# Twelve sign rows per head in place of 64 one-hot pattern rows in a bucketed attention kernel

## The chip, the core and the metric

The kernel runs on one core of a Trainium2 chip. The metric is the device time of one execution in microseconds. Three runs of the kernel before gave 800.62 us as their median (800.1 to 803.21).

## The reference

Attention with a hash mask, then a mixture of experts on its output. Query and key of a head are projected on six vectors; the signs make a bucket number, and a query sees the keys of its own bucket only. A query that finds no key in its bucket has every score at -1e9, and so the softmax is the mean over all keys.

```python
batch, n_heads, seq, head_dim = (4, 8, 768, 64)
q_bits = (einsum('bhsd,dk->bhsk', q, proj) > 0)      # 6 bits
k_bits = (einsum('bhsd,dk->bhsk', k, proj) > 0)
mask = q_bucket[:, :, :, None] == k_bucket[:, :, None, :]
scores = where(mask, scale * q @ k.T, -1000000000.0)
attn = exp(scores - max) / (sum + 1e-09)
out = attn @ v
# then the experts: route every row to its best one of 8, relu(x @ w1[e]) @ w2[e], times the gate
```

## The kernel before

The 32 heads go in 16 pairs (`NPR`); two heads share most instructions. Every pair needs four operand tiles per head, 128 rows by 768 columns: `m1` and `s1` (in 64 of the rows the rounded query or key, in the other 64 the mask rows) and `m2` and `s2` (the rounded values and the residues that the rounding left). A score is two matmuls into one bank: `s1` by `m1` (product and mask together) and `s2` by `m2` (the cross terms), lines 301 and 302 in `scores`. Three sets of operand tiles (`gens`) go round.

While pair i is scored, three other things are woven into TensorE's order. `maxp(i+1)` (lines 240 and 246) multiplies `s1` by `m1` of the next pair once without the residues, VectorE takes the maximum over the keys (lines 242, 248), and `maxp_back` (lines 269 to 272) transposes the maxima back and adds them to the mask rows of `m1`. `turn(i+2)` (line 175) transposes query and key of the pair after the next into a `psx` bank, ScalarE rounds them into `m1` (line 182), VectorE takes the residues (line 190), one ScalarE copy (line 193) and three DMAs (lines 194 to 196) bring them to the other rows. `signs(i+2)` projects on the six vectors: eight matmuls (line 208) of 384 columns into four row groups of a bank, and one VectorE comparison per half makes the bits (line 210). `patterns(i+2)` turns the bits into 64 rows: for each half and head one bf16 matmul by the constant `pat` (line 223), then a copy into the 64 mask rows of `m1` (line 224, on VectorE or ScalarE) and a ScalarE Relu into those of `s1` (line 225). A row of `m1` is then 0 where it is the query's bucket and far below zero elsewhere, a row of `s1` one-hot.

TensorE's order is written out by hand: the strings `PLAN` (six rows, one for each block of 128 keys of pair i), `PLAN0` (the first pair) and `FIRST` (before it). S is a third of the scores of a block, M a step of `maxp`, T the next step of the chain `turn`, `signs`, `patterns`, and P the last step of `patterns` of the pair before. The other queues are ordered by a scheduler. `ps_x` has two banks (`psx`), which transposes, signs, patterns and several others share. SP issues the loads and copies in order.

Of the kernel before, what the change touches and what calls it, by code (L numbers as in the profile page):

```python
# [25 lines left out]
BIG = 2.0 ** 100  # L26
CFG = dict(spd=(15,), fxs=3, wy=(0.3, 0.71), hpf=0, he=0, hn=0, hm=0, avp=(1, 2, 3, 4, 5, 6), avs=(2,), early=2, w3=(0, 0.9), x3=(0, 1), nmd=1, man=(), man0=2, hpo=0, hpe=0, p0=(0, 1), p1=(0, 0.25), p2=(0, 0.4), p3=(0.4, 0.9), s0=4, rc='DDDD', rq=(1, 2), tq=(3, 3, 1, 1, 0, 0), wh=(0.5, 0.78), ws=(0.78, 1.05), n2=2, psx=2, psm=2, pss=2, npb=6, ut=8, qk=4, v=2, wm=(0, 0.9), wf=(0.04, 1.02), wx=(0.3, 0.71), sub="DPPD", fx='D', fx3='R', raw=4, wp=7, LS=4, LL=7, pn=8, rv=(0,), rs='DDPP', r1=(0, 0.5), r2=(0, 1), avg=1, fub=2, fd=2, pm=(), fj=0, fxe=1.0)
# [4 lines left out]
    "yMSTPSMSM",  # L32
# [3 lines left out]
    "SFTTTfEMSfMSMTF",  # L36
    "fSMSMMETBABSe",
# [4 lines left out]
    "SMMSSMT",  # L42
    "TMSSMS",
    "MTMlSMBTSSMMT",
    "SABSMS",
)
FIRST = "UtmmUmtmmmttmtmUtmtnnnnbnUbnUnUnUnbUUb"


def host_consts():  # L50
    beta = (np.arange(64)[None, :] >> np.arange(6)[:, None]) & 1
    pat = np.zeros((128, 2, 128), np.float32)
    for h in range(2):
        r = 64 * h
        pat[r:r + 6, h, 0:64] = (2 * beta - 1) * BIG
        pat[r + 6, h, 0:64] = 6 * BIG
        pat[r + 32:r + 38, h, 64:128] = 2 * beta - 1
        pat[r + 38, h, 64:128] = 4
    return {
        "c_pat": pat,  # L60
        "c_id": np.eye(128, dtype=np.float32),
        "c_tri": np.triu(np.ones((128, 128), np.float32), 1),
    }
# [20 lines left out]
def attention(ctx, actx, tc, a, x_d, l_d, route=None, setup=None, before_last=None):  # L84
# [51 lines left out]
    pat = const.tile([P, 2, P], BF16, name="pat")  # L136
    pat32 = sm.tile([P, 2, P], F32, name="pat32", bufs=1)
    nc.sync.dma_start(out=pat32, in_=a["c_pat"])
    zst = const.tile([P, 32], F32, name="zst")
    nc.gpsimd.memset(zst, 0.0)  # L140
    bits = []
    for j in range(2):
        bt = const.tile([P, S], BF16, name=f"bits{j}")
        nc.gpsimd.memset(bt, 0.0)
        bits.append(bt)
    nc.vector.tensor_copy(out=zst[:, 0:6], in_=pr)
    nc.vector.tensor_copy(out=pat, in_=pat32)
# [51 lines left out]
    def signs(i, heads=(0, 1)):  # L199

        t = st[i]
        bt = bits[(i + heads[0]) % 2]
        rows = slice(64 * heads[0], 64 * heads[-1] + 64)
        for half in range(2):
            hs = slice(half * HALF, (half + 1) * HALF)
            z = ps_x.tile([P, MAIN], F32, name="psx")
            for o in range(2 * heads[0], 2 * heads[-1] + 2):
                nc.tensor.matmul(z[32 * o:32 * o + 32, 0:HALF], zst, (t["m2"], t["s2"])[o % 2][o // 2][:, hs].bitcast(F32),  # L208
                                 start=True, stop=True, tile_position=(0, 32 * o))
            nc.vector.tensor_scalar(out=bt[rows, hs], in0=z[rows, 0:HALF], scalar1=0.0, scalar2=0.5, op0=ALU.is_gt, op1=ALU.subtract)  # L210
            yield

    def patterns(i, heads=(0, 1), before=()):

        for _ in before:
            yield
        t = st[i]
        bt = bits[(i + heads[0]) % 2]
        for half in range(2):
            hs = slice(half * HALF, (half + 1) * HALF)  # L220
            for h in heads:
                pp = ps_x.tile([P, MAIN], F32, name="psx")
                nc.tensor.matmul(pp[:, 0:HALF], pat[:, h], bt[:, hs], start=True, stop=True)  # L223
                (nc.vector.tensor_copy if (half if i > 1 else i + h == 0) else nc.scalar.copy)(out=t["m1"][h][PT[h], hs], in_=pp[0:64, 0:HALF])
                nc.scalar.activation(t["s1"][h][PT[h], hs], pp[64:128, 0:HALF], AF.Relu)
                yield

    def maxp(i, late, heads=(0, 1)):
# [7 lines left out]
        for qt in range(0, NT, 2):  # L236
# [20 lines left out]
            if nh == 2:  # L257
                nm = sm.tile([P, n, 2, 64], F32R, name=f"nm{n}", bufs=2)
                nc.scalar.mul(nm, m.unsqueeze(3).broadcast_to([P, n, 2, 64]), -1.0)
            else:  # L260
                nm = sm.tile([P, n, 1], F32R, name=f"nw{n}")
                nc.vector.tensor_scalar(out=nm, in0=m, scalar1=-1.0, scalar2=None, op0=ALU.mult)
# [3 lines left out]
    def maxp_back(t, heads, rows, nm, n, cs):  # L266
# [3 lines left out]
        for h in heads:  # L270
            nc.vector.scalar_tensor_tensor(out=t["m1"][h][PT[h], cs], in0=bc[PT[h], 0:n * P], scalar=BIG / 2, in1=t["m1"][h][PT[h], cs].bitcast(F32), op0=ALU.min, op1=ALU.add)
        nc.vector.tensor_scalar(out=t["lone"][rows, cs], in0=bc[rows, 0:n * P], scalar1=BIG / 4, scalar2=None, op0=ALU.is_gt)

# [153 lines left out]
    def first():  # L427

        late = []
        for g in (turn(0, (0,)), signs(0, (0,)), patterns(0, (0,))):  # L430
            for _ in g:
                pass
        g = {"m": maxp(0, late, (0,)), "t": chain(turn(0, (1,)), signs(0, (1,)), patterns(0, (1,))),
             "n": maxp(0, late, (1,)), "U": chain(turn(1), signs(1), patterns(1))}
# [7 lines left out]
    with tc.manual_schedule(engines={mybir.EngineType.PE}):  # L442
# [17 lines left out]
        fins = xs = ts = iter(())  # L460
        late = []
        for i in range(NPR):
            ss = score(i)
            ms = maxp(i + 1, late) if i + 1 < NPR else iter(())
            last, ts = ts, chain(turn(i + 2), signs(i + 2), patterns(i + 2)) if i + 2 < NPR else iter(())
# [5 lines left out]
            for kt in range(NT):  # L471
# [5 lines left out]
                for c in (PLAN0 if i == 0 else PLAN)[kt]:  # L477
# [9 lines left out]
                    elif c == "P":  # L487
                        next(last, None)
# [607 lines left out]
```

## Time and profile before

| | |
|---|---|
| median of the runs | 800.62 us |
| the profiled execution | 806.57 us |
| its span, first to last instruction | 804.5 us |
| TensorE busy (matmul) | 770.7 us, 96% |
| VectorE, ScalarE, GpSimd busy | 63%, 52%, 51% |
| attention | to about 500 us |
| experts | the rest |

The span is some 2 us shorter than its execution's time, and that execution is 5.95 us above the median. In the rows below PE is TensorE's matmul, PEld its weight load, DVE VectorE, ACT ScalarE, POOL GpSimd, SP the sync engine, which issues most DMAs. Times within the span are in us from its start. Matmuls overlap in the pipeline, so the busy time of one (0.3 to 0.5 us) is longer than the step from one start to the next; the step is what it costs TensorE.

### The profile page before, as it was taken

What the parts mean: (1) busy time and instruction counts of PE and PEld (TensorE: products, weight loads), DVE (VectorE), ACT (ScalarE), POOL (GpSimd) and SP (SyncE); (2) the same over time, 40 slices, a digit from 0 to 9 for tenths busy, and PEclk for the clock granted to TensorE, in tenths of its full rate; (3) what the DMA queues carried; (4) which work ended last, traced back from release to release, by engine and by line L of the source; (5) the groups of instructions that cost most, each with busy time, mean ns of one, the idle gap of its engine ahead of it and who ended that gap; (6) DMA issues with size and microseconds to landing.
All of it is one profiled execution on the core that took longest, in us unless ns stands there. A gap on an engine that the chain in (4) does not pass through costs nothing.

```text
span 804.5 us, 12195 instructions
## 1 busy us (share of the span) xinstructions
PE 770.7 (96%) x4358; PEld 540.0 (67%) x4358; DVE 509.1 (63%) x944; ACT 417.8 (52%) x758; POOL 410.8 (51%) x325
## 2 busy tenths in 40 slices
PE   4799999999999999899999999989999999999996
PEld 2366666666666666566666655768888877788885
DVE  4976876887777697687797668674434343343423
ACT  4466666756656666566575545324343342433424
POOL 3147776776876677777668978421230212202002
PEclk9889999999999999999999999999999999999999
DMA  6643144315245404435311225355453567333432
GB/s 141 144 99 95 41 102 119 76 43 120 63 108 145 109 19 112 113 73 131 79 31 50 60 99 184 111 144 158 157 172 117 161 229 237 123 115 118 131 90 103
DMA packets 98055, 90.86 MB, mean 113 GB/s; under 512 B 58221, under 2 KB 77293, under 8 KB 97984
## 3 DMA queue, kind: packets, MB, share of 16 engines
q1 hardware_dynamic: 92288, 75.47, 35.5%
q0 software_dynamic: 4832, 12.94, 4.6%
q10 hardware_dynamic: 864, 1.57, 0.7%
q8 instruction: 36, 0.59, 0.3%
q14 instruction: 35, 0.29, 0.1%
HBM read 59.46 MB, written 13.14 MB: 90 GB/s over the span
## 4 chain that ended last, share of the span: by engine, by line
PE 77%; issue 11%; DVE 5%; DMA 3%; ACT 2%; POOL 1%; another core or an unknown queue 1%; SPq 0%; POOLq 0%; ACTq 0%; DVEq 0%
PE psu L338 15%; PE pss L301 9%; PE pss L302 8%; PE psm L240 5%; PE hps L836 4%; PE hps L837 4%; PE hps L838 4%; PE yps L877 3%; PE yps L879 3%; PE yps L878 3%; PE psm L246 3%; PE psx L175 3%; PE psx L208 3%; PE psx L223 2%; PE psx L361 1%
## 5 line engine op out<-in xcount | busy, mean ns | idle before, releaser
L322 POOL TENSOR_TENSOR sp<-sp,pb 128x768 f32<-128x768 f32 x124 | 226.4, 1858 | 44.5 <-ACT pb L319 43.8
L242 DVE TENSOR_REDUCE mx<-psm 128x1 f32<-128x512 f32 x192 | 131.7, 687 | 13.5 <-PE psm L240 9.8
L338 PE MATMUL psu<-pb,vt 128*64 128x512 f32 (+1 forms) x768 | 134.4, 492 | 0.0
L314 ACT ACTIVATE pb<-pss 128x512 f32<-128x512 f32 x192 | 113.0, 598 | 38.4 <-PE pss L302 29.5
L784 DVE TENSOR_TENSOR w<-raw,w 128x1024 fp32r<-128x1024 f32 x52 | 68.1, 1309 | 100.6 <-ACT w L780 77.5
L319 ACT ACTIVATE pb<-pss 128x512 f32<-128x512 f32 x96 | 57.3, 597 | 86.9 <-PE pss L302 78.1
L780 ACT CAST w<-raw 128x1024 fp32r<-128x1024 f32 x56 | 58.6, 1048 | 78.0 <-PE yps L879 78.0
L338 PEld LDWEIGHTS psu<-pb,vt 128*64 128x64 f32 x768 | 50.9, 136 | 71.4 <-issue 63.2
L322 POOL TENSOR_TENSOR sp<-pb,pb 128x768 f32<-128x768 f32 x31 | 57.0, 1860 | 57.4 <-ACT pb L319 57.4
L877 PE MATMUL yps<-w,hl 128*128 128x512 f32 x200 | 79.5, 397 | 1.3 <-DVE tslot L683 1.3
L946 POOL DMA_INDIRECT out<-y,tb x25 | 24.8, 992 | 107.0 <-ACT y L945 102.1
L879 PE MATMUL yps<-w,hh 128*128 128x512 f32 x200 | 78.2, 391 | 0.0
L878 PE MATMUL yps<-w,hh 128*128 128x512 f32 x200 | 77.9, 389 | 0.1
L301 PE MATMUL pss<-m_0g,s_0g 128*128 128x512 f32 x192 | 73.0, 380 | 3.8 <-ACT pb L314 3.4
L836 PE MATMUL hps<-xh,w 128*128 128x512 f32 x192 | 75.5, 394 | 0.6 <-DVE hl L842 0.6
L837 PE MATMUL hps<-xl,w 128*128 128x512 f32 x192 | 74.9, 390 | 0.0
L838 PE MATMUL hps<-xh,w 128*128 128x512 f32 x192 | 74.7, 390 | 0.0
L841 ACT ACTIVATE hh<-hps 128x512 fp32r<-128x512 f32 x48 | 28.6, 598 | 86.3 <-PE hps L838 77.7
L301 PE MATMUL pss<-m_1g,s_1g 128*128 128x512 f32 x192 | 69.7, 363 | 0.4 <-ACT pb L319 0.4
L248 DVE TENSOR_REDUCE mx<-psm 128x2 f32<-128x512 f32 x96 | 66.0, 688 | 5.1 <-PE psm L246 2.7
L800 POOL DMA_INDIRECT xg<-x_d,tb x17 | 17.8, 1047 | 99.2 <-DMA tb<-tab 95.6
L842 DVE SCALAR_TENSOR_TENSOR hl<-hps,hh 128x512 fp32r<-128x512 f32 x48 | 33.2, 691 | 53.3 <-ACT hh L841 50.6
(251 smaller groups left out, 1582.7 us busy)
## 6 DMA issues: line engine op xcount, KB each, us to landing
raw<-moe_w SPq DMA_DIRECT2D x56, 512.0 KB, 4.3
qk<-q SPq DMA_DIRECT2D x32, 192.0 KB, 3.7
qk<-k SPq DMA_DIRECT2D x32, 192.0 KB, 4.3
vt<-v SPq DMA_DIRECT2D x16, 384.0 KB
s_0g<-m_0g SPq DMA_DIRECT2D x30, 192.0 KB, 4.0
s_1g<-m_1g SPq DMA_DIRECT2D x30, 192.0 KB, 3.4
x_d<-xs SPq DMA_DIRECT2D x18, 256.0 KB, 2.0
tw<-moe_w SPq DMA_DIRECT2D x2, 2048.0 KB, 9.5
```

Of the source, the lines that this page charges most:

```text
L242: nc.vector.tensor_reduce(out=mx[:, qt + j, hi, 0:1], in_=mp, axis=AX.X, op=ALU.max)
L301: nc.tensor.matmul(out, t["s1"][h][:, ks], t["m1"][h][:, cs], start=True, stop=False)
L314: marks["p"] = nc.scalar.activation(pb[:, h, 0:MAIN], sp, AF.Exp, scale=0.125).ins
L322: (nc.vector if h and i in CFG["spd"] else nc.gpsimd).tensor_tensor(out=t["sp"][:, h], in0=(t["pb"][0] if kt == 1 else t["sp"])[:, h], in1 ...
L338: marks["u", kt] = nc.tensor.matmul(t["u"][part][64 * h:64 * h + 64, 0:w], t["v"][:, h, kt], t["pb"][kt][:, h, COLS[part]], start=False, s ...
L784: (nc.gpsimd if n < 8 and n % 2 else nc.vector).tensor_tensor(out=lo, in0=r, in1=hi.bitcast(F32), op=ALU.subtract)
L836: nc.tensor.matmul(hps, lo[:, c, fs], xh[:, c], start=(c == 0), stop=False)
L837: nc.tensor.matmul(hps, hi[:, c, fs], xl[:, c], start=False, stop=False)
L838: nc.tensor.matmul(hps, hi[:, c, fs], xh[:, c], start=False, stop=(c == 3))
L877: nc.tensor.matmul(yps[g], hl[fc][:, gs], hi[:, fb], start=(fc == 0), stop=False)
L878: nc.tensor.matmul(yps[g], hh[fc][:, gs], lo[:, fb], start=False, stop=False)
L879: nc.tensor.matmul(yps[g], hh[fc][:, gs], hi[:, fb], start=False, stop=(fc == 7))
```

## The change

The one-hot rows go. A mask row is now made from one sign: the projection has twelve columns instead of six (for the queries the negated and the plain vectors, for the keys the plain and the negated), the comparison on VectorE uses a threshold and a factor per row (`thr`), and gives -2^100 or 0 for a query row, 1 or 0 for a key row. The product of the twelve rows is then -2^100 times the number of bits in which query and key differ. The comparison writes a float tile `mask`, whose twelve rows per operand are brought to rows 0 to 11 of the mask half of `m1` and `s1`: from the second pair on by four DMAs on SP's queue per pair, in the first pair by ScalarE and GpSimd copies. The other 52 mask rows of `s1` are zeroed once by GpSimd at the start. `patterns` with its matmuls and evictions is gone, and the letters for its steps with it (three T and the P per pair, and four U and two t in `FIRST`). `maxp_back` adds a sixth of the maximum to twelve rows.

```diff
-    "yMSTPSMSM",
+    "yMSTSMSM",
...
-    "SFTTTfEMSfMSMTF",
-    "fSMSMMETBABSe",
+    "SFTTfEMSfMSMF",
+    "fSMSMMEBABSe",
...
-FIRST = "UtmmUmtmmmttmtmUmtnnnnbnUbnUnUnUnbUUb"
+FIRST = "UtmmUmtmmmtmtmUmnnnnbnUbnUnnnbb"
...
+    for role in range(2):
+        nc.vector.tensor_scalar(out=zst[:, role, 0:6], in0=pr, scalar1=2.0 * role - 1.0, scalar2=None, op0=ALU.mult)
+        nc.vector.tensor_scalar(out=zst[:, role, 6:12], in0=pr, scalar1=1.0 - 2.0 * role, scalar2=None, op0=ALU.mult)
+    masks = [const.tile([P, S], F32, name=f"mask{j}") for j in range(2)]
+    for g in (2, 0, 1):
+        for h in range(2):
+            nc.gpsimd.memset(gens[g]["s1"][h].bitcast(F32)[64 * h:64 * h + 64], 0.0)
...
-            nc.vector.tensor_scalar(out=bt[rows, hs], in0=z[rows, 0:HALF], scalar1=0.0, scalar2=0.5, op0=ALU.is_gt, op1=ALU.subtract)
+            nc.vector.tensor_scalar(out=mask[rows, hs], in0=z[rows, 0:HALF], scalar1=thr[rows, 0:1], scalar2=thr[rows, 1:2], op0=ALU.is_gt, op1=ALU.mult)
+            if i == 0:
+                for h in heads:
+                    to = slice(64 * h, 64 * h + NB)
+                    nc.scalar.copy(out=t["m1"][h][to, hs], in_=mask[to, hs])
+                    nc.gpsimd.tensor_copy(out=t["s1"][h][to, hs], in_=mask[64 * h + 32:64 * h + 32 + NB, hs])
+            if i > 0 and half:
+                for h in heads:
+                    for x, n in ((1, "s1"), (0, "m1")):
+                        r = 64 * h + 32 * x
+                        nc.sync.dma_start(out=t[n][h].bitcast(F32)[64 * h:64 * h + NB], in_=mask[r:r + NB])
             yield
-
-    def patterns(i, heads=(0, 1), before=()):
...
-            for h in heads:
-                pp = ps_x.tile([P, MAIN], F32, name="psx")
-                nc.tensor.matmul(pp[:, 0:HALF], pat[:, h], bt[:, hs], start=True, stop=True)
-                (nc.vector.tensor_copy if (half if i > 1 else i + h == 0) else nc.scalar.copy)(out=t["m1"][h][PT[h], hs], in_=pp[0:64, 0:HALF])
-                nc.scalar.activation(t["s1"][h][PT[h], hs], pp[64:128, 0:HALF], AF.Relu)
-                yield
...
-                nc.scalar.mul(nm, m.unsqueeze(3).broadcast_to([P, n, 2, 64]), -1.0)
+                nc.scalar.mul(nm, m.unsqueeze(3).broadcast_to([P, n, 2, 64]), -1.0 / 6)
...
-            nc.vector.scalar_tensor_tensor(out=t["m1"][h][PT[h], cs], in0=bc[PT[h], 0:n * P], scalar=BIG / 2, in1=t["m1"][h][PT[h], cs].bitcast(F32), op0=ALU.min, op1=ALU.add)
+            to = slice(64 * h, 64 * h + NB)
+            nc.vector.scalar_tensor_tensor(out=t["m1"][h][to, cs], in0=bc[to, 0:n * P], scalar=BIG / 16, in1=t["m1"][h][to, cs].bitcast(F32), op0=ALU.min, op1=ALU.add)
```

Line numbers of the kernel after the change differ by a few: its line 207 is line 208 of before, 234 is 240, 240 is 246, 296 and 297 are 301 and 302, 193 to 195 are 194 to 196.

First place, TensorE, a pair in the steady state, from the last of the sign matmuls on. Before (`bits` are the bits of the pair after the next, `pss` scores, `psm` the next pair's `maxp`):

```order
L208 MATMUL psx<-s_1g_131,zst 32x384
L223 LDWEIGHTS pat
L223 MATMUL psx<-bits_177,pat 128x384
L240 MATMUL psm<-s_0g_115,m_0g_113 128x512
L301 MATMUL pss<-m_1g_103,s_1g_105 128x512
L302 MATMUL pss<-m_1g_107,s_1g_109 128x512
L246 MATMUL psm<-s_0g_115,m_0g_113 128x256 x2
```

And now:

```order
L207 MATMUL psx<-s_1g_131,zst 32x384
L234 MATMUL psm<-s_0g_115,m_0g_113 128x512
L296 MATMUL pss<-m_1g_103,s_1g_105 128x512
L297 MATMUL pss<-m_1g_107,s_1g_109 128x512
L240 MATMUL psm<-s_0g_115,m_0g_113 128x256 x2
```

Nothing takes the place of the pattern matmul; the other three of the pair (after a later M, after the M of the row's end, and P in the next pair's first row) go in the same way.

Second place, SP's queue in the same pair, from the last copies of `turn` on. Before (each row with what it waits for):

```order
L196 DMA s_1g_131<-m_1g_125 64x768 [waits DMAHW2_49,Activation_49]
L115 DMA qk<-q 128x6x64 [waits DMAHW3_49,PE_49]
L115 DMA qk<-k 128x6x64 [waits DMAHW4_49]
L115 DMA qk<-q 128x6x64 [waits DMAHW5_49,PE_49]
L194 DMA m_0g_106<-m_0g_102 64x768 [waits DMAHW6_49,Activation_49]
```

And now:

```order
L195 DMA s_1g_131<-m_1g_125 64x768 [waits DMAHW2_49,Activation_49]
L115 DMA qk<-q 128x6x64 [waits DMAHW3_49,PE_49]
L115 DMA qk<-k 128x6x64 [waits DMAHW4_49]
L219 DMA s_0g_126<-mask_179 12x768 [waits DMAHW5_49,DVE_49]
L219 DMA m_0g_124<-mask_179 12x768 [waits DMAHW6_49]
L219 DMA s_1g_127<-mask_179 12x768 [waits DMAHW7_49,Pool_49]
L219 DMA m_1g_125<-mask_179 12x768 [waits DMAHW2_49,DMAHW1_49,DMAHW0_49]
L115 DMA qk<-q 128x6x64 [waits PE_49]
```

The four mask DMAs stand behind the pair's loads and ahead of the next pair's first load; the first of them waits for VectorE's comparison.

Third place, ScalarE in the first pair, from the last rounding of the first head on. Before:

```order
L225 ACTIVATE s_0g_126<-psx 64x384 x2
L182 CAST m_0g_102<-psx 128x512
L182 CAST m_1g_125<-psx 128x512
L184 CAST s_1g_131<-psx 64x512
```

And now:

```order
L181 CAST m_0g_102<-psx 128x512
L181 CAST m_1g_125<-psx 128x512
L213 CAST m_0g_124<-mask_178 12x384 x2
L183 CAST s_1g_131<-psx 64x512
```

Two copies of the mask rows stand behind the roundings of the next transposes, where two Relus stood ahead of them.

## Rows read from the trace of the kernel before

**Rows 1.** The page's first part: busy us, share of the span, instructions.
```profile
PE 770.7 (96%) x4358; PEld 540.0 (67%) x4358; DVE 509.1 (63%) x944; ACT 417.8 (52%) x758; POOL 410.8 (51%) x325
```
**Rows 2.** Stretches: length, each engine's busy us (count), granted clock, DMA share, GB/s.
```profile
114.50:142.00 27.50, 27.39 (x172) 17.55 (x171) 20.62 (x38) 18.68 (x37) 20.13 (x14) 1.00 0.36 88
...
311.00:339.00 28.00, 25.44 (x160) 17.34 (x160) 21.51 (x45) 18.07 (x36) 23.23 (x16) 1.00 0.23 58
```
**Rows 3.** Chain of waits in one pair: start us, us, what.
```profile
139.74 0.90 PE psx L208 x8
...
140.67 0.57 DVE bits L210
...
141.28 0.32 PE psx L223
141.60 0.23 PE psm L240
...
143.24 0.18 PE psx L223
...
150.16 0.16 PE psx L223
```
**Rows 4.** Timeline of TensorE there: start us, busy us, instruction.
```profile
140.36 0.49 PE L208 MATMUL psx<-s_1g,zst 128*32 128x384 f32 x1
...
140.68 0.49 PE L208 MATMUL psx<-s_1g,zst 128*32 128x384 f32 x1
...
141.30 0.53 PE L240 MATMUL psm<-s_0g,m_0g 128*128 128x512 f32 x1
141.67 0.40 PE L301 MATMUL pss<-m_1g,s_1g 128*128 128x512 f32 x1
...
148.86 0.40 PE L240 MATMUL psm<-s_0g,m_0g 128*128 128x512 f32 x1
```
**Rows 5.** Groups by line: busy us, mean ns of one, idle before it.
```profile
L225 ACT ACTIVATE s_0g<-psx 64x384 fp32r<-64x384 f32 x32 | 15.6, 488 | 10.5 <-DVE m_0g L224 10.4
...
L224 DVE CAST m_0g<-psx 64x384 fp32r<-64x384 f32 x16 | 8.7, 541 | 0.1
...
L224 ACT CAST m_0g<-psx 64x384 fp32r<-64x384 f32 x16 | 7.6, 473 | 20.0 <-issue 13.4 <-PE psx L223 6.6
```
**Rows 6.** Timeline of SP's queue: start us, us on the queue, instruction.
```profile
134.81 0.66 SPq L115 DMA_DIRECT2D qk<-k  x1
...
152.53 0.54 SPq L115 DMA_DIRECT2D qk<-q  x1
```
**Rows 7.** DMA issues: count, KB each, median us from issue to landing.
```profile
s_0g<-m_0g SPq DMA_DIRECT2D x30, 192.0 KB, 4.0
...
pr<-proj SPq DMA_DIRECT2D x2, 1.5 KB, 2.5
```
**Rows 8.** The tile s_0g: least, median and longest landing.
```profile
DMA to landing us min/median/max: 3.3/4.0/8.3
```
**Rows 9.** Chain of waits of the first stage: start us, us, what.
```profile
12.55 0.46 DVE bits L210
...
14.18 1.98 PE psx L175 x8
...
39.15 0.50 PE psx L269 x2
```
**Rows 10.** Stretches of the first stage, columns as in rows 2.
```profile
33.00:34.50 1.50, 1.16 (x11) 0.33 (x10) 1.50 (x5) 0.00 (x0) 0.20 (x1) 1.00 0.64 103
...
39.00:40.50 1.50, 1.36 (x6) 1.17 (x6) 0.84 (x3) 0.96 (x2) 0.99 (x1) 0.50 0.00 0
...
45.00:46.50 1.50, 1.50 (x11) 1.32 (x10) 1.32 (x4) 0.94 (x3) 0.23 (x1) 1.00 0.00 0
```
**Rows 11.** GpSimd by line: the memsets at the start, the copies of one line.
```profile
L144 POOL MEMSET bits<- 128x768 bf16 x2 | 1.4, 738 | 0.0
...
L188 POOL CAST s_0g<-m_0g 64x512 fp32r<-64x512 f32 (+1 forms) x2 | 1.0, 500 | 2.0 <-ACT m_0g L182 2.0
```

More of the change, by code (lines that the diff above doesn't have):

```diff
@@ L41 @@
     "TSvVMSMSMTMA",
-    "SMMSSMT",
+    "SMMSSM",
     "TMSSMS",
-    "MTMlSMBTSSMMT",
+    "MTMlSMBSSMM",
     "SABSMS",
 )
-FIRST = "UtmmUmtmmmttmtmUtmtnnnnbnUbnUnUnUnbUUb"
+FIRST = "UtmmUmtmmmtmtmUmnnnnbnUbnUnnnbb"
 def host_consts():
[L51 to L58, printed above, removed]
+    thr = np.zeros((4, 32, 2), np.float32)
+    for o in range(4):
+        query = o % 2 == 0
+        thr[o, 0:6 if query else 0, 0] = -TINY
+        thr[o, 6:6 if query else 12, 0] = -TINY
+        thr[o, :, 1] = -BIG if query else 1.0
     return {
-        "c_pat": pat,
+        "c_thr": thr.reshape(128, 2),
         "c_id": np.eye(128, dtype=np.float32),
@@ L135, in attention @@
     nc.vector.tensor_copy(out=identr, in_=ident)
[L136 to L139, printed above, removed]
+    thr = const.tile([P, 2], F32, name="thr")
+    nc.sync.dma_start(out=thr, in_=a["c_thr"])
+    zst = const.tile([P, 2, 32], F32, name="zst")
     nc.gpsimd.memset(zst, 0.0)
[L141 to L147, printed above, removed]
+    for role in range(2):
[5 more added lines that the diff above has]
+            nc.gpsimd.memset(gens[g]["s1"][h].bitcast(F32)[64 * h:64 * h + 64], 0.0)
     NPB = CFG["npb"]
@@ L201, in signs @@
         t = st[i]
-        bt = bits[(i + heads[0]) % 2]
+        mask = masks[(i + heads[0]) % 2]
         rows = slice(64 * heads[0], 64 * heads[-1] + 64)
@@ L207, in signs @@
             for o in range(2 * heads[0], 2 * heads[-1] + 2):
-                nc.tensor.matmul(z[32 * o:32 * o + 32, 0:HALF], zst, (t["m2"], t["s2"])[o % 2][o // 2][:, hs].bitcast(F32),
+                nc.tensor.matmul(z[32 * o:32 * o + 32, 0:HALF], zst[:, o % 2], (t["m2"], t["s2"])[o % 2][o // 2][:, hs].bitcast(F32),
                                  start=True, stop=True, tile_position=(0, 32 * o))
-            nc.vector.tensor_scalar(out=bt[rows, hs], in0=z[rows, 0:HALF], scalar1=0.0, scalar2=0.5, op0=ALU.is_gt, op1=ALU.subtract)
-            yield
-    def patterns(i, heads=(0, 1), before=()):
-        for _ in before:
-            yield
[L217 to L220, printed above, removed]
-            for h in heads:
-                pp = ps_x.tile([P, MAIN], F32, name="psx")
-                nc.tensor.matmul(pp[:, 0:HALF], pat[:, h], bt[:, hs], start=True, stop=True)
-                (nc.vector.tensor_copy if (half if i > 1 else i + h == 0) else nc.scalar.copy)(out=t["m1"][h][PT[h], hs], in_=pp[0:64, 0:HALF])
-                nc.scalar.activation(t["s1"][h][PT[h], hs], pp[64:128, 0:HALF], AF.Relu)
-                yield
+            nc.vector.tensor_scalar(out=mask[rows, hs], in0=z[rows, 0:HALF], scalar1=thr[rows, 0:1], scalar2=thr[rows, 1:2], op0=ALU.is_gt, op1=ALU.mult)
[9 more added lines that the diff above has]
+                        nc.sync.dma_start(out=t[n][h].bitcast(F32)[64 * h:64 * h + NB], in_=mask[r:r + NB])
+            yield
     def maxp(i, late, heads=(0, 1)):
@@ L429, in first @@
         late = []
-        for g in (turn(0, (0,)), signs(0, (0,)), patterns(0, (0,))):
+        for g in (turn(0, (0,)), signs(0, (0,))):
             for _ in g:
                 pass
-        g = {"m": maxp(0, late, (0,)), "t": chain(turn(0, (1,)), signs(0, (1,)), patterns(0, (1,))),
-             "n": maxp(0, late, (1,)), "U": chain(turn(1), signs(1), patterns(1))}
+        g = {"m": maxp(0, late, (0,)), "t": chain(turn(0, (1,)), signs(0, (1,))),
+             "n": maxp(0, late, (1,)), "U": chain(turn(1), signs(1))}
         for c in FIRST:
@@ L464, in attention @@
             ms = maxp(i + 1, late) if i + 1 < NPR else iter(())
-            last, ts = ts, chain(turn(i + 2), signs(i + 2), patterns(i + 2)) if i + 2 < NPR else iter(())
+            ts = chain(turn(i + 2), signs(i + 2)) if i + 2 < NPR else iter(())
             if i % 4 == 0 and i > 0:
```

10 lines of the change are left out of this document (5 added, 5 removed).

## The prediction

> **What bounds the kernel now.** I read the busy shares first, then stretches of one pair, then the chain of waits inside a pair, then TensorE's own timeline. The shares say TensorE, at 96%, with the others at half to two thirds [rows 1]. The stretch of one pair says it more sharply: TensorE is busy for 27.39 of 27.50 us at the full clock while VectorE, ScalarE and GpSimd have 7 to 9 us to spare (the first of [rows 2]). So in the steady state a TensorE step that goes is a step gained, and work taken from the other engines gains nothing by itself. Not every pair is so full: the stretch from 311 to 339 us has 2.56 us without a matmul (the second of [rows 2]), the widest hole I found in the attention, and a shorter order may only widen it.
>
> Inside a pair the chain runs along TensorE from end to end and leaves it in one place: after the eight sign matmuls it goes to VectorE's comparison and back to the first pattern matmul [rows 3]. That is the one wait that the patterns bring.
>
> **The pattern matmuls.** Each pair has four. Three stand in the chain with 0.18, 0.18 and 0.16 us (the second of these reads like the first) [rows 3], together 0.52. The first costs more, because it needs the comparison of what was just projected. The last sign matmuls start at 140.68, the M behind at 141.30 and the score behind that at 141.67 [rows 4], 0.99 us in all. Without the pattern the M could start one pass after 140.68; a pass starts 0.32 us behind the one ahead of it (140.36 and 140.68 [rows 4]), so that would be 141.00, and the M itself is a step of 0.23 [rows 3]. So 0.99 - 0.32 - 0.23 = 0.44 us goes with the first pattern; I take 0.42, for the last pass may end a little late. A pair gains 0.52 + 0.42 = 0.94 us, and the 14 pairs whose patterns lie in the steady state gain 13.2 us. The bounds: at least the bare step of 0.16 for each of the four, 0.64 a pair or 9.0 us; at most the whole wait and all pieces, 0.57 + 0.32 + 0.52 = 1.41 a pair or 19.7 us. I take 13.2, since the starts of the very matmuls around the place give it.
>
> The Trainium skill ("TensorE: Matmul & The Clock Gate", section "Wait — 56ns, not 53.3ns?") gives a warm matmul its column count over 2.4 GHz plus 2.5 ns; as an estimate from that page a pattern of 384 columns is 0.1625 us, 56 of them 9.1 us, and the total by it 790. The trace agrees on the three later patterns (0.16 to 0.18 us) and shows 0.42 on the first, which the page's figure doesn't hold because it is mostly a wait.
>
> **What leaves ScalarE and VectorE.** Per pair four Relus of 0.488, two copies on ScalarE of 0.473, two on VectorE of 0.541 [rows 5]: 2.9 and 1.1 us. They lie beside TensorE's work, which is busy 27.39 of 27.50, so I cost them at nothing. The comparison keeps its 384 columns and its bank; that it reads a threshold per row and writes four bytes instead of two I cost at nothing as well, for it now has until the masks are needed. Two fewer users of the `psx` banks can only help transposes and signs, again worth nothing where TensorE doesn't wait for them.
>
> **What is added: four DMAs per pair and their wait.** The new path from comparison to the first M of the pair runs through SP and the DMA engines. Before, the comparison starts at 140.67 and takes 0.57 for each of its halves [rows 3], so it ends at about 141.8. SP has nothing to do then: its last load was issued at 134.81 and the next waits until 152.53 [rows 6], so the DMAs wait there for VectorE and hold up nothing but that load, which comes 8 us later. An issue takes some 0.5 us, so `s1` and `m1` of the first head go at 141.85 and 142.35, of the second at 142.9 and 143.4. The first M on them stands at 148.86 before [rows 4], 147.9 after a gain of 0.94. For landing, a 1.5 KB DMA took 2.5 us and a 192 KB one 4.0 [rows 7]; a mask DMA is 36 KB, so I take 2.5 to 4.0, nearer the lower. `m1` of the first head lands at 144.9 to 146.4, 1.5 to 3 us early. Hidden, at zero. The cover ends where a landing takes over 5.6 us; the longest on that tile was 8.3 [rows 8], and there it would cost 150.65 - 147.9 = 2.7 us.
>
> **The first stage, to 39 us.** It is a chain through all engines, not TensorE's. Bits, pattern, copy, Relu, then eight transposes that wait for the Relu to free a bank, at 14.18 [rows 9]. Now the comparison frees the bank: the first four transposes can follow the sign matmuls, which overlap the comparison that the chain shows at 12.55 [rows 9], and the next four come at its end, about 13.1; the second head is rounded some 1 to 1.8 us earlier. Behind it ScalarE has two mask copies of 0.47 (the price of a 384-column copy, [rows 5]) ahead of the second head's other copies, so 0.8 us is left for these. VectorE's maxima come with them, and then VectorE has no room (1.50 of 1.50 us in a stretch at 33 us [rows 10]), so little more is gained; the two small gaps where it waited for patterns go. I take 1.5 us off the 39.15 at which the scores begin [rows 9], bounds 0 (VectorE sets all of it) and 3 (all of 12.55 to 14.18 and as much again for the second head). GpSimd's six memsets at 0.74 each instead of two [rows 11] add 3 us at the start, where everything waits for the first loads; if its own first copies come later for it, they are needed by the maxima only, behind the transposes of 14.18 [rows 9]. Zero, and 3 us if that cover were gone. Its mask copies, four of about 0.5 [rows 11], run beside ScalarE's. The masks of the second pair go through DMAs and are needed some 4 to 5 us after their comparison, by my estimate from the order of the rows and the durations above: 0 to 1 us of wait, inside the bounds.
>
> **Sum.** 13.2 + 1.5 = 14.7 us. The profiled execution took 806.57, its successor would take 791.9; from the median of 800.62, 785.9, said as 786.0.
>
> **The rivals.** First, the masks land a little late. Landings near 6.1 us would cost 0.5 us a pair, 7 us over 14 pairs, and give 793. For it speaks that the loads of the next pairs use the same DMA engines; against, that SP has issued the last of them 7 us earlier [rows 6]. 12 in 100.
>
> Second, the other side: the masks land so late that the kernel is slower. One mechanism: `maxp` of the next pair waits at its first M, once in each pair. It decides from landings of 6.6 us (1 us a pair, all that the patterns gave); at 7.0 us it gives 806, at 8.3 us 824. Only the longest landing seen reaches it, and that for five times the bytes. 4 in 100.
>
> Third, the clock. From 39 to 45 us TensorE ran dense at a granted clock of 0.50, that is 1.2 GHz, and at 1.00 from 45 on [rows 10]: 6 us that cost 3. Ahead of it TensorE was thinly busy, and the change takes matmuls from just that stretch. A second slow stretch as long costs 3 us, 789; if the slow stretch falls elsewhere or goes, 3 us are gained, 783. 13 in 100 for both. The Trainium skill's page on TensorE (section "What's actually happening") says that the gate's default is throttled and that activity releases it; by that rule less work in the first stage speaks for 789. The trace agrees that a dense stretch ended the slow one, and shows no change's effect on it.
>
> Fourth, TensorE waits in places for ScalarE, and 4 us less on ScalarE and VectorE per pair lets it catch up: about 4 us of the holes close, 782. For it speak holes such as the second of [rows 2]; against, that TensorE is full in most pairs. 7 in 100.
>
> Fifth, nothing moves: the steps saved turn up as waits, for scores, GpSimd's sums or the residue DMAs set the pace of a pair. 800. Against it speak 27.39 of 27.50 us. 4 in 100.
>
> **How the numbers follow.** The forecast has 60 in 100 and its own range is 783 to 790. The range runs from the upper bounds of the first stage with a better clock (13.2 + 3 + 3 = 19.2, 781) to the lower bound of the steady state, nothing in the first stage and a worse clock (9.0 + 0 - 3 = 6.0, 794.6, cut to 794); the late masks at 793 lie in it. A measurement of this kernel can tell about 0.5% or 4 us from no change. Faster by more: all but the second and fifth, 0.92; the same 0.04; slower 0.04.
>
> **What would show it.** Right: no row of pattern matmuls; TensorE 26.4 to 26.6 us per pair and still as full; scores begin at 37 to 38 us; the mask DMAs land in 2.5 to 4 us, and no M of a pair's first row waits for a DMA. Wrong: an idle time of the M in a pair's first row released by a mask DMA (first and second rival); the clock at 0.50 past 45 us (third); pairs of 27.4 us with more idle time in TensorE (fifth).

## The result, and the profile after

The changed kernel took 791.85 us (median of four runs, 791.06 to 793.02), the kernel before on the same chip 800.36: a ratio of 0.9888, interval 0.986 to 0.9915. So 8.5 us were gained. The forecast was 786.0, that is 14.7 us, with a range of 781 to 794: the sign and the place were right, and the sum was 6 us too large. Five further runs of it (e1) gave 790.91 against 799.96. The medians and ratios here leave out one execution each of the kernel before (1919.98 us), of e11 (1246.9) and of e12 (986.46), all far off.

The first view is the busy shares of the kernel after, the line that answers to [rows 1].

```profile
PE 761.1 (96%) x4294; PEld 532.8 (67%) x4294; DVE 492.8 (62%) x916; ACT 376.7 (48%) x664; POOL 415.7 (53%) x333
```

The 64 pattern matmuls are gone (4358 to 4294), and TensorE is as full as before. VectorE lost 16 us and ScalarE 41.

Next, two stretches of it, with the columns of [rows 2]: one plain pair, and four microseconds in the seventh pair.

```profile
112.00:138.66 26.66, 26.55 (x167) 16.74 (x165) 19.13 (x35) 15.89 (x30) 19.89 (x14) 1.00 0.40 95
...
224.00:228.00 4.00, 3.55 (x13) 1.25 (x13) 1.36 (x3) 0.00 (x0) 4.00 (x3) 0.61 0.23 57
```

A plain pair takes 26.66 us, 0.7 less than before, and is full; 26.4 to 26.6 were forecast. The second row is a surprise: TensorE waited there for data, and then its granted clock fell to 0.61 in the mean of the stretch, so part of it ran at 1.2 GHz.

TensorE's timeline behind the sign matmuls, which answers to [rows 4] (start us, busy us, instruction):

```profile
137.88 0.49 PE L207 MATMUL psx<-s_1g,zst 128*32 128x384 f32 x1
...
138.21 0.49 PE L207 MATMUL psx<-s_1g,zst 128*32 128x384 f32 x1
138.62 0.50 PE L234 MATMUL psm<-s_0g,m_0g 128*128 128x512 f32 x1
138.96 0.39 PE L296 MATMUL pss<-m_1g,s_1g 128*128 128x512 f32 x1
139.19 0.40 PE L297 MATMUL pss<-m_1g,s_1g 128*128 128x512 f32 x1
```

From the last pass (138.21) to the score behind the M (138.96) it takes 0.75 us (0.75 or 0.76 in the other plain pairs). Before it was 0.99, so 0.23 went, not the 0.42 of my sum. I had let the M follow one pass later, after 0.32, and take 0.23. It follows after 0.41 to 0.42 and takes 0.34: the first matmuls behind a block of sign matmuls are each about 0.1 us slow. Before, the M took as long (0.37, from 141.30 to 141.67), so that part of the 0.99 did not go with the pattern.

The mask DMAs on SP's queue, by destination (shortest, median and longest ns on the queue, first and last start us):

```profile
L219 SPq DMA_DIRECT2D s_0g<-mask x15: 781/817/921, 35.5 to 425.7; - x15
L219 SPq DMA_DIRECT2D m_0g<-mask x15: 781/797/812, 36.5 to 426.6; - x15
L219 SPq DMA_DIRECT2D s_1g<-mask x15: 713/714/726, 37.3 to 427.5; - x15
L219 SPq DMA_DIRECT2D m_1g<-mask x15: 715/725/863, 38.1 to 428.3; - x15
```

An issue takes 0.71 to 0.82 us at the median, not some 0.5. No matmul of this run was released by one of them. When a mask DMA landed can be read in the trace from the last update of its semaphore: in the second profile (e1) 54 of the 60 landed 2.2 to 2.5 us after their issue, and the longest took 3.9.

Where the gain went is best read from the length of each pair. I take from the timelines the start of the first matmul of each pair's weighing (the `psu<-lone` matmul), for the kernel before (its second profile, e5 below) and for the kernel after (its second profile, e1 below):

| stretch | before, us | after, us | gained |
|---|---|---|---|
| up to the first weighing | 48.73 | 47.32 | 1.41 |
| five plain stretches (2, 3, 6, 10, 12), mean | 27.92 | 27.17 | 0.75 |
| 1, 8 and 14 | 83.61 | 81.18 | 2.43 |
| with routing work: 5 and 13 | 59.47 | 58.47 | 1.00 |
| with a new wait of 0.27 us for an exp: 4 and 9 | 57.06 | 56.44 | 0.62 |
| where x is stored: 7 and 11 | 61.00 | 60.58 | 0.42 |
| the last (15) | 25.32 | 25.32 | 0.00 |

The 14 stretches that lost their patterns gained 8.2 us where I had forecast 13.2. The same sum from the two profiles first taken is 9.2; it flatters the change, since that profile of before had a hole in TensorE (the second of [rows 2]) that did not come again: the stretch with it took 31.19 us there and 28.54 in the second profile.

### The profile page after: what moved, and what is told of

Read it like the earlier page. It is cut to its first block, busy times and chain, and to the rows that moved or that the text cites. A ratio compares the mean times of both kernels' runs of the same rounds, so it can differ in the third digit from the quotient of the medians.

```text
span 791.2 us, 12125 instructions
## 1 busy us (share of the span) xinstructions
PE 761.1 (96%) x4294; PEld 532.8 (67%) x4294; DVE 492.8 (62%) x916; ACT 376.7 (48%) x664; POOL 415.7 (53%) x333
## 4 chain that ended last, share of the span: by engine, by line
PE 79%; issue 10%; DMA 5%; DVE 2%; ACT 2%; POOL 1%; SPq 0%; POOLq 0%; ACTq 0%; DVEq 0%
PE psu L333 14%; PE pss L296 9%; PE pss L297 8%; PE psm L234 6%; PE hps L829 5%; PE hps L830 5%; PE hps L831 5%; PE yps L870 4%; PE yps L872 4%; PE yps L871 4%; PE psx L207 4%; PE psm L240 3%; PE psx L174 3%; DMA s_1g<-m_1g 2%; PE psx L356 1%
## 5 line engine op out<-in xcount | busy, mean ns | idle before, releaser
L317 POOL TENSOR_TENSOR sp<-sp,pb 128x768 f32<-128x768 f32 x124 | 225.8, 1849 | 39.5 <-ACT pb L314 38.9
L309 ACT ACTIVATE pb<-pss 128x512 f32<-128x512 f32 x192 | 114.8, 600 | 79.3 <-PE pss L297 71.1
L777 DVE TENSOR_TENSOR w<-raw,w 128x1024 fp32r<-128x1024 f32 x52 | 66.2, 1274 | 101.2 <-ACT w L773 101.1
L314 ACT ACTIVATE pb<-pss 128x512 f32<-128x512 f32 x96 | 57.3, 597 | 88.3 <-PE pss L297 85.4
```

Source lines behind the costliest of these rows:

```text
L309: marks["p"] = nc.scalar.activation(pb[:, h, 0:MAIN], sp, AF.Exp, scale=0.125).ins
L317: (nc.vector if h and i in CFG["spd"] else nc.gpsimd).tensor_tensor(out=t["sp"][:, h], in0=(t["pb"][0] if kt == 1 else t["sp"])[:, h], in1 ...
L777: (nc.gpsimd if n < 8 and n % 2 else nc.vector).tensor_tensor(out=lo, in0=r, in1=hi.bitcast(F32), op=ALU.subtract)
```

## Experiments

**e1: the same kernel again.** No edit; the yardstick for the next three.

> The changed kernel once more, unaltered, as the yardstick for the three runs beside it. Expected: about 792 us, 8.5 us less than the kernel before. Two readings of its profile differ in one place. If the loss of 1.4 us in the pair between 217 and 246 us belongs to the kernel, this profile shows again a pair of about 33 us there, with sign matmuls waiting for the residue DMAs and the granted clock below 1.00. If it belonged to that one execution, the pair takes about 31 us.

It took 790.91 us (790.42 to 792.77), 0.9897 of before. Two rows of its TensorE timeline in the seventh pair:

```profile
221.88 0.83 PE L207 MATMUL psx<-m_1g,zst 128*32 128x384 f32 x2 [0.79 <-DMA m_1g<-m_1g]
223.52 0.51 PE L207 MATMUL psx<-s_1g,zst 128*32 128x384 f32 x1 [0.81 <-DMA s_1g<-m_1g]
```

The wait for the residue DMAs came again, 1.6 us, and the fall of the clock did not: the pair took 31.06 us where the first profile had 32.83. The kernel before waits there as well (1.19 us for the same DMA). So the wait belongs to both kernels, and the fallen clock to that one execution.

**e2 to e4: putting the patterns back in parts.**

> The changed kernel with the four pattern matmuls per pair put back at their old places in TensorE's order (pairs 2 to 15), but reading a constant zero tile and with nobody reading their result: only their steps, no wait and no eviction. Theory 1, which I now hold: the old first pattern cost only about 0.23 us, because it hid two small switches behind the sign matmuls, and the three others 0.52. Then the bare steps cost 3 x 0.17 + 0 to 0.17 = 0.52 to 0.68 us per pair, 7.3 to 9.5 us over 14 pairs: 799 to 801.5. Theory 2, the prediction's sum with something else taking 0.2 us per pair: four steps of 0.16 to 0.18, 9.5 us: 801.5. This run alone is the base for the next one.

> As the run before, but the pattern matmuls load their weights from the mask tile that the comparison has just written, so the first of them waits for VectorE as the old one did. Results are still unread. Theory 1: the wait adds only 0.05 to 0.2 us per pair to the bare steps, 0.72 to 0.75 us per pair in all, 10 to 10.5 us: about 802. Theory 2: the first pattern with its wait costs 0.42 and the four cost 0.94 as predicted, 13.2 us: about 805.

> As the run before, and the results are evicted as in the kernel before, per half and head one copy (ScalarE for the first half, VectorE for the second) and one Relu on ScalarE, into scratch tiles that nobody needs. That puts 2.9 us of ScalarE and 1.1 us of VectorE work back into each pair. Theory 1, as predicted (relief of ScalarE and VectorE is worth nothing): within 1 us of the run before. Rival (their relief closes holes): about 4 us slower than the run before.

The lines of e4; e2 and e3 end with the matmul, and e2 has `gz[:, 0:P]` for the mask's upper halves:

```diff
+    def ghost(i):
...
+            for h in range(2):
+                pp = ps_x.tile([P, MAIN], F32, name="psx")
+                nc.tensor.matmul(pp[:, 0:HALF], masks[i % 2].bitcast(BF16).rearrange("p (s two) -> p s two", two=2)[:, half * HALF:half * HALF + P, 1], gz, start=True, stop=True)
+                (nc.vector.tensor_copy if half else nc.scalar.copy)(out=masks[(i + 1) % 2][PT[h], hs] if half else scr[PT[h]], in_=pp[0:64, 0:HALF])
+                nc.scalar.activation(scr[PT[h]], pp[64:128, 0:HALF], AF.Relu)
```

e2 took 800.86 us, e3 801.35, e4 809.31. So the four matmuls alone are worth at most 10 us against e1, and 13.2 is refuted. By the profiles of e1 and e2, 8.6 us of it lie in the 14 stretches, 0.61 each; 1.1 lie ahead of the first weighing, where e2 has no patterns, and the rest in the experts. But e2 did not do what I said: its first pattern waited too.

```profile
113.22 0.32 PE L230 MATMUL psx<-gz 128*128 128x384 bf16 x1 [0.23 <-DVE mask L211]
```

It needs one of the two `psx` banks, and both hold the halves of the projection until the comparison frees one. The wait that I had put down to data comes from the bank as well, and e2 and e3 tell nothing of its price; e12 was made for that.

e4 is 8 us slower than e3, which looks as if the relief of ScalarE were worth that. Its ScalarE queue in a plain pair, and TensorE's row that waited:

```profile
116.53 0.47 ACT L232 CAST scr<-psx 64x384 fp32r<-64x384 f32 x1
117.03 0.60 ACT L323 ACTIVATE pb<-pss 128x512 f32<-128x512 f32 x1
117.65 0.49 ACT L233 ACTIVATE scr<-psx 64x384 fp32r<-64x384 f32 x1
...
118.19 0.53 PE L277 MATMUL psx<-identr,nm 128*128 128x128 f32 x4 [0.28 <-ACT scr L233]
```

An exp stands between the copy and the Relu of one pattern and holds the bank 0.6 us longer, in 11 of the 14 pairs. In the kernel before it stands there in none of them. It came from my scratch tile: copy and Relu wrote the same rows, and so the scheduler put something between them.

**e6: the evictions in the old order.**

> As the run with patterns and evictions in the call before, but the Relu writes other rows than the copy, so that on ScalarE's queue no exp slips between the two, as in the kernel before. In that run one exp ahead of the Relu held a bank 0.6 us longer in most pairs, and TensorE waited for it. Theory 1 (ScalarE's and VectorE's relief is worth nothing, that run lost to the one place in the queue): about 801.5 us, within 1 us of the run with patterns and their wait. Rival (relief is worth 4 us and more): 805 to 809.

```diff
-                nc.scalar.activation(scr[PT[h]], pp[64:128, 0:HALF], AF.Relu)
+                nc.scalar.activation(scr[QK[h]], pp[64:128, 0:HALF], AF.Relu)
```

803.52 us: 2.2 more than e3, 5.8 less than e4. The plain stretches 2 and 3 are equal in e6 and e3 (27.41 and 27.42 us in both), where e4 has 27.95 and 27.97. What e6 has more lies ahead of the first weighing (1.1 us, where nothing was put back), in the first stretch (0.9) and in the eleventh, where x is stored (1.1). So 4 us of the other engines' work per pair are worth nothing in a plain pair, as predicted, and 5.8 of e4's 8 us were one exp in the wrong place. The time lies between what the two theories gave. In the first stretch the relief is worth something: it takes 28.33 us before, 28.79 in e6, but 27.85 in e3 with patterns and no evictions, and 27.47 in e1 with neither, so about half of its gain of 0.86 is relief.

**e12: the first pattern moved away from its wait.**

> As the run with the four bare pattern matmuls, which took 1.0015 of the kernel before. There the first of them turned out to wait 0.23 us all the same, for its bank, which the comparison has to free. Here that first one stands one M and one score later, when the bank is free, so it waits for nothing; the other three are unchanged. Theory 1: the wait cost nothing, since behind the sign matmuls the next M starts late anyway, and a pattern costs its step wherever it stands: within 1 us of that run, 1.0005 to 1.003 of the kernel before. Theory 2: the wait of 0.23 us is what the first pattern cost; without it 14 pairs gain 0.15 to 0.23 us each, 2.1 to 3.2 us: 0.9975 to 0.999 of the kernel before.

```diff
-    "SFTTTfEMSfMSMTF",
+    "SFTTfEMSTfMSMTF",
```

799.34 us, 0.9986 of before (0.9969 to 1.0003), where e2 had 1.0015 (1.0003 to 1.0027): 2.3 us for 14 pairs, 0.17 each. The two intervals just meet; the stretches decide. A plain pair takes 27.22 to 27.24 us instead of 27.39 to 27.41. Theory 2 holds here: the wait did cost something. With 26.65 as the plain pair without patterns, four bare steps cost 0.58 and the wait 0.17, 0.75 together. My terms were 0.52 for three steps and 0.42 for the first with its wait; measured are 0.58 for four and 0.17 for the wait. This split is e2's and not that of the kernel before. e2 keeps the new comparison, 0.12 us longer than the old one (e5), and its first pattern waits 0.23 us where the old one waited 0.11 (the last sign matmul ends at 141.17 by [rows 4], the pattern starts at 141.28 by [rows 3]). From the last pass to the score e2 takes 1.11 us, so its first pattern costs 0.35 and the other three 0.39 together; before it was 0.23 and 0.52. That a plain pair is as long in both is in part luck. The Trainium skill ("TensorE: Matmul & The Clock Gate", section "Wait — 56ns, not 53.3ns?") makes it 0.65 for the four, as an estimate from its figure; the trace agrees within 0.07. The total by that page, 790, was nearer to 791.85 than mine, in part by luck, for it takes 14 equal pairs too.

**e5: the comparison alone, and a second profile of before.**

> The kernel before, with 32 VectorE comparisons of 384 columns from one bank put behind its end, eight each of four forms: bf16 output with fixed scalars (the old form), 4-byte output with fixed scalars, bf16 output with scalars per row, and 4-byte output with scalars per row (the new form). The old line took 0.558 us at the median, the new one 0.676. If the wider output costs it, forms 2 and 4 take about 0.68 and form 3 0.56; if the scalars per row cost it, forms 3 and 4 take 0.68. The rest is a second look at the kernel before: the hole of 2.45 us in TensorE at 329 us and the first pair of about 48.7 us belong to the kernel if they come again; I expect the first pair again and the hole not.

```diff
+        for _ in range(8):
+            nc.vector.tensor_scalar(out=b16, in0=z[:, 0:HALF], scalar1=0.0, scalar2=0.5, op0=ALU.is_gt, op1=ALU.subtract)
...
+            nc.vector.tensor_scalar(out=b32, in0=z[:, 0:HALF], scalar1=row[:, 0:1], scalar2=row[:, 1:2], op0=ALU.is_gt, op1=ALU.mult)
```

The groups of the four forms on VectorE (busy us, mean ns of one, idle before it), then the line of the kernel after:

```profile
L1095 DVE TENSOR_SCALAR b<-yps,row 128x384 bf16<-128x384 f32 x8 | 5.4, 676 | 0.3
L1097 DVE TENSOR_SCALAR b<-yps,row 128x384 f32<-128x384 f32 x8 | 5.4, 676 | 0.3
L1091 DVE TENSOR_SCALAR b<-yps 128x384 bf16<-128x384 f32 x8 | 4.5, 557 | 0.3
L1093 DVE TENSOR_SCALAR b<-yps 128x384 f32<-128x384 f32 x8 | 4.4, 556 | 0.2
```
```profile
L209 DVE TENSOR_SCALAR mask<-psx,thr 128x384 f32<-128x384 f32 x30 | 19.5, 674 | 13.5 <-PE psx L207 12.9 <-POOL tri L567 0.5
```

The scalars per row cost 0.12 us, the wider output nothing. The forms differ in their second operation too (subtract and mult), which was not varied by itself. That the mult costs the 0.12 doesn't fit line 381 of the kernel after: a comparison and a mult with fixed scalars, 48 columns, 0.197 us, where line 267, one comparison with a fixed scalar (0.424 us for 256 columns, 0.692 for 512), gives an estimate of 0.206 for 48. In the steady state VectorE has that time. The second profile has the first weighing at 48.73 us (48.69 in the first profile), and no hole.

**e7 and e9: the sign matmuls later.**

> The changed kernel, with the eight sign matmuls of each pair four to five places later in TensorE's order of the fifth row (behind two M and two S, the second half behind one more M), about 1.4 us. Theory 1: in the pairs that also store x (the seventh and the eleventh) the sign matmuls waited 1.6 and about 1.4 us for the residue DMAs, and that wait goes: 788 to 789 us, those two pairs about 29.5 and 28.1 us, and the others unchanged. Rival 1: the residue DMAs are later still, because they wait behind the store and the loads, and the gain is under 1 us: 790 to 791. Rival 2: the masks now come too late for the first M of the next pair; 0.5 us per pair would make it 797.

> The changed kernel, with the eight sign matmuls later, and undivided, only in the seventh and the eleventh pair (those that store x and prepare a further pair); the other pairs as before. Theory: the run with all signs later gained 2.9 and 1.4 us in those two pairs (28.11 and 28.14 us instead of 31.06 and 29.52) and lost 0.33 us and more in the others, because the divided block costs TensorE a second slow start behind it. Undivided, those two take about 27.8 us and nothing is lost elsewhere: 786 to 787 us. Rival: the residue DMAs move with everything else and the two pairs keep 29 us or more: 789 to 791.

```diff
-    "SFTTfEMSfMSMF",
+    "SFfEMSfMSTMTF",
...
-                for c in (PLAN0 if i == 0 else PLAN)[kt]:
+                for c in ("SFfEMSfMSTTMF" if kt == 4 and i in (6, 10) else (PLAN0 if i == 0 else PLAN)[kt]):
```

The first change is e7's, the second e9's.

e7 took 794.7 us (793.25 to 799.64), 0.9957 of before (0.9935 to 0.9978), slower than the unaltered kernel. The seventh and eleventh stretch shrank to 28.11 and 28.14 us as expected, and the plain ones (2 and 3) grew from 26.65 to 26.97. TensorE's timeline shows why, in a plain pair between and behind the two halves:

```profile
112.40 0.49 PE L207 MATMUL psx<-s_1g,zst 128*32 128x384 f32 x1
112.82 0.49 PE L234 MATMUL psm<-s_1g,m_1g 128*128 128x512 f32 x1
113.24 0.51 PE L207 MATMUL psx<-m_0g,zst 128*32 128x384 f32 x1
...
113.61 0.49 PE L207 MATMUL psx<-s_1g,zst 128*32 128x384 f32 x1
114.02 0.50 PE L296 MATMUL pss<-m_0g,s_0g 128*128 128x512 f32 x1
114.36 0.40 PE L297 MATMUL pss<-m_0g,s_0g 128*128 128x512 f32 x1
```

The slow start (0.41 to 0.42 to the next matmul, 0.34 to 0.42 for that one) is now paid twice. That is the effect that made my first-pattern term wrong, seen by itself. The second rival holds in places too: in the sixth stretch an M waited 0.4 us for `m_1g` from `mask`, and in the fourteenth, which grew by 1.8 us, the same M waited 1.3 us. Why the fifth, the ninth and the thirteenth grew by 0.5 us each I did not follow up.

e9 took 788.98 us (788.0 to 789.16), 0.9862 of before (0.9839 to 0.9885), some 2 us under e1. The two stretches take 28.48 and 28.42 us, 3.7 less together, though not the 27.8 that I expected, and the others stay within 0.2; 1 us of it is hidden by a slower first stage in that profile. All five runs lie below all of e1's, but the intervals of the two ratios just overlap (e1: 0.9882 to 0.9912), so the 2 us are likely and not certain. e10 below, with the same row, has 0.9864 (0.984 to 0.9887). The residue DMAs are a limit of both kernels in these two pairs, and a faster pair leaves them less time: stretches 7 and 11 gained 0.4 us together from the change, instead of 1.5.

**e8 and e10: the first stage.**

> The changed kernel, with two bf16 matmuls on a zero tile ahead of each n in the later part of the first stage, 24 or so in all, into a bank that is free there; nobody reads them. Theory (clock): TensorE's thin stretch ahead of 39 us lets the granted clock fall to 0.50 for about 3 us of dense work; kept busy it stays at 1.00 and the first pair's chain ends 1 to 1.5 us earlier: 789.5 to 790. Rival: the first stage is set by VectorE's maxima and the clock has no share in it, or the clock falls anyway: 791 to 792.

> As the run before, and in the first pair the mask rows of m1 are copied by GpSimd too, not by ScalarE, where they stood behind the second head's roundings and held the first M until 15.53 us. Theory 1: the first M comes at about 14.3 us, VectorE's maxima start 1.2 us earlier, and as VectorE is full from there to 38 us the scores begin 0.8 to 1.2 us earlier: 785 to 786. Rival: the first stage is held by the roundings and GpSimd's own copies further on, nothing is gained: same as the run before, 786 to 787.

```diff
+            if k > 16 and c == "n":
+                for _ in range(2):
+                    nc.tensor.matmul(fill, gz[:, 0:P], gz, start=True, stop=True)
...
-                    nc.scalar.copy(out=t["m1"][h][to, hs], in_=mask[to, hs])
+                    nc.gpsimd.tensor_copy(out=t["m1"][h][to, hs], in_=mask[to, hs])
```

The first change is e8's, the second e10's, which has e9's row as well.

e8 took 790.75 us, the same as e1. Its clock fell all the same where the first stage ends (columns as in [rows 2]):

```profile
38.00:39.50 1.50, 0.70 (x3) 0.74 (x4) 0.82 (x3) 0.00 (x0) 0.57 (x1) 0.66 0.32 54
39.50:41.00 1.50, 1.50 (x6) 1.10 (x6) 0.85 (x3) 0.60 (x1) 0.00 (x0) 0.50 0.34 68
```

The theory fails as I tried it: 16 matmuls (not the 24 that I had counted) ahead of 36 us did not hold the clock through the two microseconds behind them, in which TensorE waited for VectorE. Whether work in just that gap would is left open.

In e10 the first M starts at 14.23 us instead of 15.63 (e9), and nothing comes of it: the scores begin at 39.54 and 39.51, the time is 788.91 and 788.98. The rows of e10 at the end of the stage:

```profile
36.40 0.44 PE L263 MATMUL psx<-identr,nw 128*128 128x128 f32 x4
39.27 0.47 PE L263 MATMUL psx<-identr,nw 128*128 128x128 f32 x2 [2.44 <-DVE nw L256]
39.54 0.76 PE L296 MATMUL pss<-m_0g,s_0g 128*128 128x512 f32 x1
```

TensorE waits 2.44 us for VectorE's last maxima. A lead of 1.4 us on ScalarE and TensorE at 14 us is lost on the way there; VectorE ends the stage at the same time. Whether VectorE alone sets the stage is not shown by it, for the clock differed too. From 20 to 24 us, e9 and then e10 (columns as in [rows 2]):

```profile
20.00:24.00 4.00, 3.66 (x9) 1.27 (x8) 3.27 (x8) 2.28 (x5) 0.39 (x1) 1.00 0.89 183
20.00:24.00 4.00, 3.38 (x8) 0.98 (x7) 2.99 (x7) 1.69 (x4) 0.26 (x1) 0.50 0.41 71
```

In e10 TensorE ran at 1.2 GHz there and VectorE was idle for 1.01 us (0.73 in e9), so part of the lead may have gone to the clock.

**e11: the mask DMAs doubled.**

> The changed kernel, with a second copy behind each of the 60 mask DMAs, from the same twelve rows to rows of the other mask tile that nobody uses. SP's queue then carries eight issues of 0.7 to 0.8 us in each pair, and the last mask row is issued some 3 us later. Theory (as predicted: the mask DMAs are hidden, and SP has room): within 1 us of the changed kernel, 790 to 792, and no M released by a mask DMA. Rival 1: SP's queue is part of what was lost; four more issues cost 0.3 us per pair: 795. Rival 2: the cover is thinner than predicted, M's of the second head wait for the mask rows that come 3 us later: 1 us per pair, 805.

```diff
                         nc.sync.dma_start(out=t[n][h].bitcast(F32)[64 * h:64 * h + NB], in_=mask[r:r + NB])
+                        nc.sync.dma_start(out=masks[(i + 1) % 2][r + NB:r + 2 * NB], in_=mask[r:r + NB])
```

791.66 us, 0.8 us more than e1 and 0.99 of before (0.9877 to 0.9923). By the time alone the first theory holds; the trace says otherwise. The first M of the second head waits in the sixth, the tenth and the fourteenth stretch. SP's issue of the last mask row in the sixth, and then TensorE's rows of that M in the sixth and fourteenth:

```profile
200.17 0.71 SPq L219 DMA_DIRECT2D m_1g<-mask  x1
```
```profile
208.13 0.47 PE L235 MATMUL psm<-s_1g,m_1g 128*128 128x512 f32 x1 [2.70 <-DMA m_1g<-mask]
...
435.28 0.47 PE L235 MATMUL psm<-s_1g,m_1g 128*128 128x512 f32 x1 [0.96 <-DMA m_1g<-mask]
```

In the tenth the profile puts the wait down to VectorE, but the last update of that mask DMA's semaphore comes at 322.51 and the M starts at 322.60. These three are the pairs in which GpSimd issues the six small scatters of the routing table (197.78 to 208.78 us in the first of them). The last mask row there landed 7.8, 6.3 and 5.8 us after its issue. In e7, where nothing is doubled but this row is also issued later (201.87 and 429.01), it took 6.1 and 6.7 us in the sixth and the fourteenth stretch. In the unaltered kernel (e1) the same row of the sixth stretch was issued ahead of the first scatter (197.71), and its M:

```profile
197.27 0.72 SPq L219 DMA_DIRECT2D m_1g<-mask  x1
```
```profile
204.92 0.47 PE L234 MATMUL psm<-s_1g,m_1g 128*128 128x512 f32 x1
```

It landed after 3.3 us, 4.3 us ahead of the M; in the tenth and fourteenth stretch it took 2.3 and 2.2. So the row is late where it is issued some 3 us later, beside the scatters; how they hold it up is open. The sixth stretch took 32.65 us instead of 27.76, for behind the wait the granted clock fell once more (0.60 from 208 to 212 us). The stretches behind two of the three, 7 and 11, got back 3.2 and 1.5 us, because the residue DMAs had the time in which TensorE waited. So my second rival's mechanism exists, in three pairs of 14, once the rows are issued 3 us later. The kernel as changed had 4.3 us to spare in the sixth stretch of e1.

## Why the prediction was right, and its sum too large

- **TensorE bounds the pair, and only its own steps count.** Right in the plain pairs: they are full before and after, e6 shows that the evictions beside them cost nothing there, and e4 what they cost once one of them holds a bank too long. The first stretch is the exception (some 0.5 us of relief, e6).
- **The pattern matmuls, 0.94 a pair.** The step that failed is "without the pattern the M could start one pass later and is a step of 0.23". I took both steps from other places of the timeline; behind the sign matmuls they are 0.42 and 0.34. So the first pattern was worth 0.23 instead of 0.42, and a plain pair 0.75. That is 2.7 us of the 6.
- **14 equal pairs.** The second failing step: I multiplied one pair's price by 14. Six stretches gave less: the two with routing work 0.5 each, because there the first pattern had waited for nothing (0.88 us from the last pass to the score before, so it was worth 0.12, as in 7, 9 and 11) and the second stood ahead of transposes (0.14 where a plain pair has 0.30); two lost some 0.27 us to a new wait for an exp (in the fourth the profile names it, in the ninth the score starts at 279.01, just behind the end of an exp at 278.97; why that exp comes late I could not settle, and the ninth also has routing work); the two that store x, because the sign matmuls wait for residue DMAs there. Together with 0.2 us that stretches 1, 8 and 14 gained more, that is the other 2.3 us of 13.2 - 8.2.
- **The first stage, 1.5 us off 39.15.** The third term that was mis-sized, within its bounds. 39.15 is the last transposes of the stage; the scores begin at 39.44 and 39.58 us in the two profiles of before, and at 39.55 and 38.90 in those of after. In the ten traces that have this first stage (five of them with one more memset) they begin at 38.9 to 40.1, 39.4 in the mean, so little more than 0.1 us of the gain is the stage's. The first weighing comes at 47.3 to 48.9 us, 48.0 in the mean, 0.7 earlier than before; the rest of that goes with the clock (below). The stretches of e10 fit my lower bound (VectorE sets all of it) but don't show it. The comparisons there are 0.12 us longer each, which I had costed at nothing. The term is some 0.8 us of the 6.
- **The mask DMAs, hidden.** Right, and the landings nearly so: 2.2 to 2.5 us mostly and 3.9 at the longest (e1), where I had 2.5 to 4. Two things were off. The issue was 0.7 to 0.8 us and not 0.5, and beside the scatters, which I had not weighed at all, a row issued 3 us later landed after 5.8 to 7.8 us (e11).
- **The clock.** My third rival's gaining side came in small, and it isn't in the sum. Before, TensorE ran at a granted clock of 0.50, 1.2 GHz, from the first score to about 45 us in both profiles; after, it was back at 1.00 sooner in both. The second profile of before (e5) and of after (e1):

```profile
42.00:45.00 3.00, 3.00 (x13) 2.53 (x12) 1.74 (x3) 1.78 (x3) 0.00 (x0) 0.52 0.00 0
```
```profile
42.00:45.00 3.00, 3.00 (x21) 2.66 (x21) 2.97 (x6) 2.35 (x6) 1.47 (x2) 1.00 0.22 76
```

The 40 matmuls from the first score to the first weighing took 9.26 and 9.15 us before and 8.74 and 8.43 after, 0.6 less in the mean; why the clock rose sooner is open. Ahead of 39 us two executions of the same kernel differ: from 24 to 27 us the granted clock is 0.52 in the first profile of after and 0.92 in the second. e2 had 1.00 from 21 to 39 us and its first weighing at 48.39, later than e1 at 47.32 with 0.50 from 21 to 24: there the clock did not set the time. Behind a wait in a full stretch it did: the seventh pair of the first profile took 1.8 us more than in e1, 0.2 of them wait, and the sixth of e11 some 2.2 beside its wait. The 1.6 us of waits in e1 brought no fall.

## What to carry to other kernels

Price a removed instruction by what stands behind it after the removal, not by steps taken from elsewhere: an engine may be slow at the start of the next kind of work, and that start stays. Multiply a price by the number of places only after looking at each kind of place, above all those where a DMA's landing was just in time. An eviction that nobody waits for still sets when its bank comes free, so one instruction ahead of it on its queue can cost the bound engine its whole length.

## What I had not expected of the hardware

- A VectorE comparison of 384 columns from a bank took 0.676 us with scalars per row and 0.557 with fixed ones, whatever the output's width (e5).
- Behind a block of 4-byte sign matmuls in four row groups the next two matmuls started about 0.1 us later each (0.42 and 0.34 instead of 0.32 and 0.23), and dividing the block in two paid it twice, 0.32 us a pair (e7).
- A DMA of twelve rows from one tile to another kept SP's queue 0.71 to 0.82 us at the median; one of 64 rows (lines 194 to 196 of before) 0.46 to 0.59 at the median.
- A 36 KB DMA landed 2.2 to 2.5 us after its issue nearly always (e1), and 5.8 to 7.8 us when it was issued beside GpSimd's small scatters (the last mask row, e7 and e11).
